# A dense GELU layer with its gradients: w1's second part issued earlier, dummy products in the head, and the first block's outputs taken out in another order

## The chip, the cores and the metric

The kernel runs on one core of a Trainium2 chip. TensorE multiplies matrices into PSUM, VectorE and ScalarE work on tiles, GpSimd and SyncE issue most transfers; all of them run side by side and wait for each other through semaphores. The metric is the device time in microseconds (us) of one execution. The kernel before takes 278.68 us, the median of three runs (277.06 to 278.73).

## The reference

All arrays are bf16: x and grad_out are 2048 x 448, w1 is 448 x 1792, w2 is 1792 x 448, with biases b1 and b2.

```python
def _fwd_reference(x, w1, b1, w2, b2):
    h = jnp.einsum("bsd,df->bsf", x, w1) + b1
    h = _gelu(h)                                  # tanh approximation
    return jnp.einsum("bsf,fd->bsd", h, w2) + b2

_out, _vjp = jax.vjp(_f, x, w1, b1, w2, b2)
_grads = _vjp(grad_out)
return (_out, *_grads)
```

So there are six outputs: the layer's result, and the gradients of x, w1, b1, w2 and b2.

## The kernel before, in words

The rows are cut into four blocks of 512, the 1792 hidden columns into seven pairs of 128. The main loop (line 371) has 28 steps, `g` = 0 to 27, seven for each block; a step handles one pair in one block, with rows along the free axis.

For a step, `M1` (line 216) multiplies w1 by x into `u` in PSUM: six matmuls of 512 columns, three for each half of the pair. 448 is three times 128 and 64 more, and the products of these 64 are in `rest` (line 227), which runs them for `u` of the next step and for `q` of this one, in the order u, q, u, q. `M4` (line 240) is the other six matmuls of `q`, w2 transposed by grad_out. `act_first` (line 246) copies `u` with its bias to `V` (line 250), squares it (line 251) and takes the GELU to `hT` (line 252). `dve_first` (line 266) makes an argument for `act_second`'s tanh (line 270), `dve_second` (lines 274 to 277) builds the derivative of the GELU, and `dve_gate` (line 280) multiplies it with `q` into `ghT`. `u` and `q` have one buffer each. So M1 of a step can start when ScalarE has copied the step before, and `q` can be written when the gate before has read it.

The order of everything is written out by hand. Step 0 is prepared ahead of the loop: lines 365 to 370 are M1(0), its remainder, `first_step`, which shares step 0 between ScalarE and VectorE, and M1(1). In the loop, step g runs `rest` for g + 1 and g, M4(g), the gate, the first half of step g + 1, and then pieces of products that make outputs.

These products are `Unit`s (line 293): kind "o" is 128 rows of the layer's result, kind "g" 128 rows of x's gradient. A unit is fourteen matmuls of 448 columns (line 311), one for each 128 hidden columns, run as pieces between the other work. Its accumulator is one of four PSUM buffers `acc` taken in a ring. Block 0's four "o" units grow in steps 0 to 6, two pieces each a step (`grown`). Block 1's first two "o" units grow in steps 7 to 13; in these steps block 0's "g" units run too (`own`, eight pieces a step). When a unit is full, it is taken out either by VectorE, which adds b2 (line 327), or by ScalarE (line 325); a unit that ScalarE takes out has b2 added by one more matmul (line 313), of a row of ones by one row of b2. Which engine it is, line 297 says. Step 6 ends with a `flush` for ScalarE's units; VectorE's come in the next step, behind M4 and ahead of the gate (line 380). In step 7 M1(9) stands ahead of the pieces, in the other steps M1 stands behind them.

The loads of the first weights are lines 167 to 175. SyncE issues the transposed loads of x, grad_out and w2 (lines 139, 140, 144, 145, 155, 156), ScalarE b1 and the first 512 columns of w1 in two parts (lines 148 and 149, called at 169 and 171); between these two parts stands an activation of one element (line 170) that loads ScalarE's table. Before any data is there, TensorE runs eight products of zeros (line 178), brings b1 onto partitions by fourteen small products (line 182), and runs one more product of zeros (line 185).

Behind the loop come the last block's units, then the column sums for the biases, then the gradients of w1 (lines 463 and 471) and w2 (line 482), which are nothing but matmuls and copies.

Of the kernel before, what the change touches and what calls it, by code (L numbers as in the profile page):

```python
# [10 lines left out]
BF16 = mybir.dt.bfloat16  # L11
# [7 lines left out]
def kernel(  # L19
# [15 lines left out]
    nc = tc.nc  # L35
    P = 128
    B, S, D = x.shape
# [23 lines left out]
    const = ctx.enter_context(tc.tile_pool(name="const", bufs=1))  # L61
# [22 lines left out]
    T_flat = const.tile([P, 4 * 2 * SB], BF16, name="T")  # L84
    b2_bc = const.tile([P, D], BF16, name="b2_bc")
    b1_col = const.tile([P, NF], F32, name="b1_col")
    ones_r = const.tile([1, P], BF16, name="ones_r")

    w1_sb = w1_flat.rearrange("p (k f) -> p k f", k=KD)
    w2T_sb = w2T_flat.rearrange("p (k f) -> p k f", k=KD)  # L90
# [8 lines left out]
    def xq(b):  # L99
        o = (b % 2) * 2 * KD * SB  # L100
        return xg_flat[:, o:o + KD * SB].rearrange("p (k s) -> p k s", k=KD)

    def gq(b):
        o = ((b % 2) * 2 + 1) * KD * SB
        return xg_flat[:, o:o + KD * SB].rearrange("p (k s) -> p k s", k=KD)
# [5 lines left out]
    def hT(g):  # L111
        return ring(hT_flat, HR, g)

    def ghT(g):
        return ring(ghT_flat, GR, g)
# [21 lines left out]
    def load_x(b):  # L137
        rows = slice(b * SB, (b + 1) * SB)
        nc.sync.dma_start_transpose(out=xq(b)[:, 0:KF, :], in_=x2[rows, DL:D])
        nc.sync.dma_start_transpose(out=xq(b)[:, KF, :], in_=x2[rows, 0:P])  # L140

    def load_g(b):
        rows = slice(b * SB, (b + 1) * SB)
        nc.sync.dma_start_transpose(out=gq(b)[:, KF, :], in_=g2[rows, DOV:D])
        nc.sync.dma_start_transpose(out=gq(b)[:, 0:KF, :], in_=g2[rows, 0:DM])

    def load_w1(eng, f0, f1):
        eng.dma_start(out=w1_sb[:, 0:KF, f0:f1], in_=w1[DL:D, f0:f1].rearrange("(k p) f -> p k f", p=P))
        eng.dma_start(out=w1_sb[0:DL, KF, f0:f1], in_=w1[0:DL, f0:f1])
# [13 lines left out]
    b1_row = T_flat[0:1, 4 * SB:4 * SB + F]  # L163
    nc.vector.memset(warm, 0.0)
    nc.vector.memset(ones, 1.0)
    nc.vector.memset(ones_r[:], 1.0)
    load_x(0)
    nc.scalar.dma_start(out=b1_row, in_=b1.rearrange("(o f) -> o f", o=1))
    load_w1(nc.scalar, 0, 256)
    nc.scalar.activation(out=T_flat[0:1, SB + 2:SB + 3], in_=ones, func=ACT.Gelu_apprx_tanh)  # L170
    load_w1(nc.scalar, 256, 512)
    load_g(0)
    load_w2T(0, 256)
    load_w2(nc.sync, 0, 2)
    load_w1(nc.sync, 512, 768)
    pw = psum_a.tile([P, SB], F32, name="acc")
    for i in range(8):
        nc.tensor.matmul(pw[:], lhsT=warm[:, 0:P], rhs=warm, start=True, stop=True)

    pb = psum_a.tile([P, SB], F32, name="acc")  # L180
    for ft in range(NF):
        nc.tensor.matmul(pb[:, ft:ft + 1], lhsT=b1_row[:, ft * P:(ft + 1) * P], rhs=ones, start=True, stop=True)
    nc.vector.tensor_copy(out=b1_col[:], in_=pb[:, 0:NF])
    for i in range(1):
        nc.tensor.matmul(pw[:], lhsT=warm[:, 0:P], rhs=warm, start=True, stop=True)
    load_w2T(256, 512)
    load_w2(nc.sync, 2, 4)
# [18 lines left out]
    def blk(g):  # L206
        return divmod(g, NPAIR)

    def cols(g, h):
        c = g % NPAIR  # L210
        return slice((2 * c + h) * P, (2 * c + h + 1) * P)
# [4 lines left out]
    def M1(g):  # L216
        if g == 0:
            u_of[g] = [psum_a.tile([P, SB], F32, name="acc")[:] for h in range(2)]
        else:
            u = psum_u.tile([P, 2, SB], F32, name="u")  # L220
            u_of[g] = [u[:, h, :] for h in range(2)]
        for h in range(2):
            for kt in range(KF):
                nc.tensor.matmul(u_of[g][h], lhsT=w1_sb[:, kt, cols(g, h)], rhs=xq(g // NPAIR)[:, kt, :],  # L224
                                 start=(kt == 0), stop=False, skip_group_check=True)

    def rest(gu, gg):

        if gg is not None:
            q = psum_g.tile([P, 2, SB], F32, name="q")  # L230
            g_of[gg] = q
        for h in range(2):
            if gu is not None:
                nc.tensor.matmul(u_of[gu][h], lhsT=w1_sb[0:DL, KF, cols(gu, h)], rhs=xq(gu // NPAIR)[0:DL, KF, :],  # L234
                                 start=False, stop=True, tile_position=(0, 0), skip_group_check=True)
            if gg is not None:
                nc.tensor.matmul(q[:, h, :], lhsT=w2T_sb[DL:P, KF, cols(gg, h)], rhs=gq(gg // NPAIR)[DL:P, KF, :],
                                 start=True, stop=False, tile_position=(DL, 0), skip_group_check=True)

    def M4(g):  # L240
        for h in range(2):
            for kt in range(KF):
                nc.tensor.matmul(g_of[g][:, h, :], lhsT=w2T_sb[:, kt, cols(g, h)], rhs=gq(g // NPAIR)[:, kt, :],  # L243
                                 start=False, stop=(kt == KF - 1), skip_group_check=True)

    def act_first(g):
        u = u_of.pop(g)
        for h in range(2):
            ft = 2 * (g % NPAIR) + h
            nc.scalar.activation(out=V_of(g)[:, h, :], in_=u[h], func=ACT.Identity, bias=b1_col[:, ft:ft + 1])  # L250
        nc.scalar.activation(out=A_of(g), in_=V_of(g), func=ACT.Square, scale=math.sqrt(3.0 * GELU_C * GELU_A))  # L251
        nc.scalar.activation(out=hT(g), in_=V_of(g), func=ACT.Gelu_apprx_tanh)  # L252
# [13 lines left out]
    def dve_first(g):  # L266
        nc.vector.scalar_tensor_tensor(out=B_of(g), in0=A_of(g), scalar=3.0 * GELU_C, in1=V_of(g), op0=ALU.add, op1=ALU.mult)  # L267
# [11 lines left out]
    def dve_gate(g):  # L279
        nc.vector.scalar_tensor_tensor(out=ghT(g), in0=t_of(g), scalar=1.0, in1=g_of.pop(g)[:], op0=ALU.add, op1=ALU.mult)  # L280
# [12 lines left out]
    class Unit:  # L293
        def __init__(self, kind, b, j):
            self.kind, self.b, self.j, self.done, self.ps = kind, b, j, 0, None

            self.by_act = kind == "g" or (b == 0 and j >= 2)

        def piece(self):
            ft = self.done  # L300
            c, h = divmod(ft, 2)
            g = self.b * NPAIR + c
            if self.ps is None:
                self.ps = psum_a.tile([P, SB], F32, name="acc")
            js = slice(self.j * P, (self.j + 1) * P)
            if self.kind == "o":
                lhsT, rhs = hT(g)[:, h, js], w2_sb[:, ft, :]
            else:
                lhsT, rhs = ghT(g)[:, h, js], w1T_sb[:, ft, :]
            bias = self.by_act and self.kind == "o"  # L310
            nc.tensor.matmul(self.ps[:, 0:D], lhsT=lhsT, rhs=rhs, start=(ft == 0), stop=(ft == NF - 1 and not bias))  # L311
            if bias and ft == NF - 1:
                nc.tensor.matmul(self.ps[:, 0:D], lhsT=ones_r[:], rhs=b2_bc[0:1, :], start=False, stop=True)
            self.done += 1
            return self.done == NF

# [18 lines left out]
    def run_pieces(units):  # L335
        for un in units:
            if un.piece():
                full.append(un)

    def flush(by_act=None):  # L340
        for un in [un for un in full if by_act in (None, un.by_act)]:
            full.remove(un)
            evict(un)
# [27 lines left out]
    for g in range(NSTEP):  # L371
        b, c = blk(g)
        pieces = [U[k] for k in seq[b] for _ in range(NF)]
        n = len(pieces)
        own = pieces[n * c // NPAIR:n * (c + 1) // NPAIR]
        grown = [U[k] for k in grow[b] for _ in range(2)]
        nxt = g + 1 if g + 1 < NSTEP else None
        rest(nxt, g)
        M4(g)
        flush(False)  # L380
        dve_gate(g)
        if nxt is not None:
            act_first(nxt)
        flush(True)
        if nxt is not None:
            dve_first(nxt)
        last = b == 0 and c == NPAIR - 1
        if last:
            run_pieces(grown + own)
            flush(True)  # L390
        if nxt is not None:
            act_second(nxt)
            dve_second(nxt)
        if g == NPAIR:
            M1(g + 2)
        if not last:
            run_pieces(grown + own)
        if g != NPAIR and g + 2 < NSTEP:
            M1(g + 2)
        for _ in range(2):  # L400
            if g >= NPAIR - 1 and stored < g:
                store_h(stored)
                stored += 1
        if c == 2 and 0 < b < NB - 1:
            load_x(b + 1)
            load_g(b + 1)
        for t in turns.get(g, []):
            turn_gh(*t)
# [45 lines left out]
    for t0, t1 in ((0, 4), (4, HT)):  # L454
        n = (t1 - t0) * P
        for h in range(2):
            a0, a1 = t0 + h * HT, t1 + h * HT
            cs = slice(a0 * P, a1 * P)
            for kt in range(KF):
                ps = psum_a.tile([P, SB], F32, name="acc")  # L460
                psv = ps[:, 0:n].rearrange("p (t f) -> p t f", f=P)
                for st in range(NS):
                    nc.tensor.matmul(psv, lhsT=x_all[:, st, kt * P:(kt + 1) * P], rhs=gh_rows(st, a0, a1),  # L463
                                     start=(st == 0), stop=(st == NS - 1))
# [3 lines left out]
        for st in range(NS):  # L468
            for h in range(2):
                psv = ps[h * DL:(h + 1) * DL, 0:n].rearrange("p (t f) -> p t f", f=P)  # L470
                nc.tensor.matmul(psv, lhsT=x_all[:, st, KF * P:D], rhs=gh_rows(st, t0 + h * HT, t1 + h * HT),  # L471
                                 start=(st == 0), stop=(st == NS - 1), tile_position=(0, h * DL), skip_group_check=True)
# [49 lines left out]
```

## Time and profile before

| | |
|---|---|
| median of three runs | 278.68 us (277.06 to 278.73) |
| the profiled execution, its own time | 278.49 us |
| its span from first to last instruction | 276.7 us |
| granted TensorE clock, mean | 0.993 |
| TensorE busy | 269.0 us, 97% |
| VectorE busy | 189.0 us, 68% |
| ScalarE busy | 144.2 us, 52% |
| GpSimd busy | 50.7 us, 18% |

Times inside the profile are counted from the span's start. PE is TensorE's matmuls, PEld its weight loads, DVE VectorE, ACT ScalarE, POOL GpSimd, SP SyncE; a "q" behind a name is the engine's queue of transfers. A matmul's end is modelled and overlaps the start of the next, so the distance between two starts is the better measure of what one costs.

### The profile page before, as it was taken

Reading aid. Unit: us, or ns where it says so; the run is one execution under the profiler, and the core shown is the slowest. Engines: PE = TensorE matmul, PEld = TensorE weight load, DVE = VectorE, ACT = ScalarE, POOL = GpSimd, SP = SyncE. Lnnn points to the kernel's source line nnn. Section 1 sums busy time; section 2 is a strip of 40 time slices with the busy share of each in tenths; the row PEclk is TensorE's granted clock in tenths of the full one; section 3 lists DMA queues with packets and bytes.
Section 4 is the critical chain, followed back from the end, with each engine's and each line's share of the span. In section 5 each row is a group of like instructions: output and inputs, shape, how many; then the busy total and the mean of one; then the engine's idle time right before and its main releaser. Section 6 shows DMA issues by size and latency. Waiting matters only on the chain.

```text
span 276.7 us, 3585 instructions
## 1 busy us (share of the span) xinstructions
PE 269.0 (97%) x1401; PEld 123.6 (45%) x1401; DVE 189.0 (68%) x218; ACT 144.2 (52%) x188; POOL 50.7 (18%) x54
## 2 busy tenths in 40 slices
PE   8799999899999999999999999999999999999994
PEld 3144443344444444444444445554444655555552
DVE  0679999999999999899888781129999980000000
ACT  2597888788878877888667750021111211112111
POOL 0000000840120503031130234211700019400000
PEclk9799999999999999999999999999999999999999
DMA  7989999999789965435635329999999961101110
GB/s 147 189 206 177 218 142 224 237 326 227 135 223 182 263 79 114 71 113 112 175 121 78 109 71 218 309 341 250 196 185 262 246 88 57 42 10 50 50 52 33
DMA packets 101763, 43.78 MB, mean 158 GB/s; under 512 B 90353, under 2 KB 98353, under 8 KB 101746
## 3 DMA queue, kind: packets, MB, share of 16 engines
q1 hardware_dynamic: 94272, 26.68, 52.6%
q0 software_dynamic: 4448, 14.69, 16.4%
q10 hardware_dynamic: 3026, 2.18, 2.9%
q8 instruction: 11, 0.18, 0.3%
q14 instruction: 6, 0.05, 0.1%
HBM read 7.00 MB, written 14.23 MB: 77 GB/s over the span
## 4 chain that ended last, share of the span: by engine, by line
PE 81%; DVE 12%; SPq 4%; DMA 1%; ACT 0%; issue 0%; DVEq 0%
PE acc L311 27%; PE acc L482 15%; PE acc L463 13%; PE q L243 10%; PE u L224 9%; PE u L234 4%; DVE Bt L267 3%; DVE T L274 3%; DVE ghT_h L280 3%; PE acc L471 2%; DVE T L277 2%; DVE T L275 1%; DMA w_gw<-in_w_dram 1%; SPq L155 1%; SPq L156 1%; DVE T L276 1%
## 5 line engine op out<-in xcount | busy, mean ns | idle before, releaser
L311 PE MATMUL acc<-w_gw,hT_h 128*128 128x448 bf16 x224 | 46.1, 352 | 0.0
L311 PE MATMUL acc<-w1T_gw,ghT_h 128*128 128x448 bf16 x224 | 45.2, 352 | 0.0
L224 PE MATMUL u<-xg_h,w_x 128*128 128x512 bf16 x162 | 40.7, 388 | 3.0 <-DMA w_x<-in_w_dram 2.0
L250 ACT ACTIVATE VA<-u,b_col 128x512 f32<-128x512 f32 x54 | 34.1, 681 | 17.3 <-PE u L234 16.6
L280 DVE SCALAR_TENSOR_TENSOR ghT_h<-T,q 128x1024 bf16<-128x1024 bf16 x28 | 34.2, 1221 | 10.8 <-PE q L243 9.7
L243 PE MATMUL q<-xg_h,w2T_g 128*128 128x512 bf16 x168 | 41.1, 381 | 0.0
L463 PE MATMUL acc<-gh_nat,w_x 128*128 128x512 bf16 (+1 forms) x192 | 36.7, 353 | 0.0
L270 ACT ACTIVATE T<-Bt 128x1024 bf16<-128x1024 f32 x28 | 29.6, 1056 | 11.8 <-DVE Bt L267 11.7
L274 DVE SCALAR_TENSOR_TENSOR T<-VA,hT_h 128x1024 bf16<-128x1024 f32 x28 | 34.1, 1218 | 0.2 <-ACT hT_h L264 0.2
L267 DVE SCALAR_TENSOR_TENSOR Bt<-VA 128x1024 f32<-128x1024 f32 x27 | 32.9, 1218 | 0.0
L311 PEld LDWEIGHTS <-hT_h 128*128 128x128 bf16 x224 | 21.8, 98 | 21.6 <-issue 0.2
L311 PEld LDWEIGHTS <-ghT_h 128*128 128x128 bf16 x224 | 21.9, 98 | 20.8
L448 DVE TENSOR_TENSOR VA<-VA,gh_nat 128x1792 f32<-128x1792 f32 x14 | 30.0, 2142 | 0.5
L251 ACT ACTIVATE VA<-VA 128x1024 f32<-128x1024 f32 x27 | 28.5, 1057 | 0.9
L252 ACT ACTIVATE hT_h<-VA 128x1024 bf16<-128x1024 f32 x27 | 28.1, 1041 | 0.0
L224 PEld LDWEIGHTS <-w_x 128*128 128x128 bf16 x168 | 16.7, 100 | 22.9 <-issue 3.5
L463 PEld LDWEIGHTS <-w_x 128*128 128x128 bf16 x192 | 18.7, 98 | 17.8 <-issue 0.4
L243 PEld LDWEIGHTS <-w2T_g 128*128 128x128 bf16 x168 | 14.1, 97 | 25.4 <-issue 12.2
L484 ACT CAST w_gw<-acc 128x448 bf16<-128x448 f32 x13 | 6.9, 533 | 32.6 <-PE acc L482 32.6
L331 POOL DMA_DIRECT2D out_dram<-io_o x8 | 6.0, 748 | 96.2 <-DVE io_o L327 48.3
L465 ACT CAST w1T_gw<-acc 128x512 bf16<-128x512 f32 (+1 forms) x12 | 6.3, 533 | 30.1 <-PE acc L463 23.9
L284 POOL DMA_DIRECT2D hT_dram<-hT_h x28 | 20.4, 729 | 0.7 <-ACT hT_h L252 0.7
(55 smaller groups left out, 230.4 us busy)
## 6 DMA issues: line engine op xcount, KB each, us to landing
hT_dram<-hT_h POOLq DMA_DIRECT2D x28, 256.0 KB, 3.9
out_dram<-io_o POOLq DMA_DIRECT2D x8, 224.0 KB, 4.6
out_dram<-io_g POOLq DMA_DIRECT2D x8, 224.0 KB, 2.9
w_x<-in_x_dram POOLq DMA_DIRECT2D x1, 1792.0 KB, 11.1
w2T_g<-in_grad_out_dram POOLq DMA_DIRECT2D x1, 1792.0 KB, 15.0
out_dram<-w_gw SPq DMA_DIRECT2D x4, 336.0 KB, 2.4
w_x<-in_w_dram SPq DMA_DIRECT2D x2, 384.0 KB, 3.7
out_dram<-w1T_gw ACTq DMA_DIRECT2D x2, 384.0 KB, 5.2
```

The source lines that it names most:

```text
L224: nc.tensor.matmul(u_of[g][h], lhsT=w1_sb[:, kt, cols(g, h)], rhs=xq(g // NPAIR)[:, kt, :], start=(kt == 0), stop=False, skip_group_check= ...
L243: nc.tensor.matmul(g_of[g][:, h, :], lhsT=w2T_sb[:, kt, cols(g, h)], rhs=gq(g // NPAIR)[:, kt, :], start=False, stop=(kt == KF - 1), skip_ ...
L250: nc.scalar.activation(out=V_of(g)[:, h, :], in_=u[h], func=ACT.Identity, bias=b1_col[:, ft:ft + 1])
L251: nc.scalar.activation(out=A_of(g), in_=V_of(g), func=ACT.Square, scale=math.sqrt(3.0 * GELU_C * GELU_A))
L267: nc.vector.scalar_tensor_tensor(out=B_of(g), in0=A_of(g), scalar=3.0 * GELU_C, in1=V_of(g), op0=ALU.add, op1=ALU.mult)
L270: nc.scalar.activation(out=t_of(g), in_=B_of(g), func=ACT.Tanh, scale=-1.0 / 3.0)
L274: nc.vector.scalar_tensor_tensor(out=p_of(g), in0=A_of(g), scalar=GELU_C, in1=hT(g), op0=ALU.add, op1=ALU.mult)
L280: nc.vector.scalar_tensor_tensor(out=ghT(g), in0=t_of(g), scalar=1.0, in1=g_of.pop(g)[:], op0=ALU.add, op1=ALU.mult)
L311: nc.tensor.matmul(self.ps[:, 0:D], lhsT=lhsT, rhs=rhs, start=(ft == 0), stop=(ft == NF - 1 and not bias))
L448: nc.vector.tensor_tensor(out=gsb_v, in0=gsb_v, in1=gh_rows(st, 0, NF), op=ALU.add)
L463: nc.tensor.matmul(psv, lhsT=x_all[:, st, kt * P:(kt + 1) * P], rhs=gh_rows(st, a0, a1), start=(st == 0), stop=(st == NS - 1))
L482: nc.tensor.matmul(ps[:, 0:D], lhsT=h_blk[ft][:, st, :], rhs=g_all[:, st, :], start=(st == 0), stop=(st == NS - 1))
```

## The change

Five edits, none of which changes what is computed.

1. The second part of w1 (columns 256 to 511) is issued by ScalarE directly behind the first; the one-element activation follows both.
2. In the head there are seven products of zeros and, behind b1, three, instead of eight and one. In step 0 four more products, of w1 by x, stand between `rest` and M4(0); nothing reads their result.
3. b2 is added by a product over all 128 partitions: a tile of 1/128 by b2 as it stands on every partition, instead of a row of ones by one row.
4. In block 0 ScalarE takes out units 0 and 1, VectorE units 2 and 3; it was the other way round.
5. In step 7 the pieces of block 1's two "o" units run ahead of M1(9), those of the "g" unit behind it; before, all ran behind it.

```diff
-    ones_r = const.tile([1, P], BF16, name="ones_r")
+    w128 = const.tile([P, P], BF16, name="w128")
...
-    nc.vector.memset(ones_r[:], 1.0)
+    nc.vector.memset(w128[:], 1.0 / P)
...
     load_w1(nc.scalar, 0, 256)
+    load_w1(nc.scalar, 256, 512)
     nc.scalar.activation(out=T_flat[0:1, SB + 2:SB + 3], in_=ones, func=ACT.Gelu_apprx_tanh)
-    load_w1(nc.scalar, 256, 512)
...
-    for i in range(8):
+    for i in range(7):
         nc.tensor.matmul(pw[:], lhsT=warm[:, 0:P], rhs=warm, start=True, stop=True)
...
-    for i in range(1):
+    for i in range(3):
         nc.tensor.matmul(pw[:], lhsT=warm[:, 0:P], rhs=warm, start=True, stop=True)
...
-            self.by_act = kind == "g" or (b == 0 and j >= 2)
+            self.by_act = kind == "g" or (b == 0 and j < 2)
...
-                nc.tensor.matmul(self.ps[:, 0:D], lhsT=ones_r[:], rhs=b2_bc[0:1, :], start=False, stop=True)
+                nc.tensor.matmul(self.ps[:, 0:D], lhsT=w128[:], rhs=b2_bc[:], start=False, stop=True)
...
         rest(nxt, g)
+        if g == 0:
+
+            for i in range(4):
+                nc.tensor.matmul(pw[:], lhsT=w1_sb[:, 0, 0:P], rhs=xq(0)[:, 0, :], start=True, stop=True)
         M4(g)
...
         if g == NPAIR:
+            run_pieces(grown)
             M1(g + 2)
-        if not last:
+            run_pieces(own)
+        elif not last:
             run_pieces(grown + own)
```

## The prediction

> **What bounds the kernel now.** I read the shares of the chain of waits first, then the chain in order of time, then TensorE's waits. Columns of the chain: start, duration, what.
>
> ```profile
> PE 81%; DVE 12%; SPq 4%; DMA 1%; ACT 0%; issue 0%; DVEq 0%
> ```
> ```profile
> 16.31 1.21 DVE Bt L267
> ...
> 45.60 1.22 DVE ghT_h L280
> ...
> 49.53 0.69 ACT VA L250
> ...
> 50.26 1.46 PE u L224 x6
> ...
> 53.98 0.32 PE u L234
> ...
> 273.18 0.53 ACT w_gw L490
> ```
> ```profile
> PE u L224 <- DMA w_x<-in_w_dram: 2.0, 1, 2.0
> PE u L224 <- ACT VA L250: 0.9, 1, 0.9
> ```
>
> The run has three parts. Up to 16.3 us is the head: loads, and step 0. From 16.3 to 49.5 VectorE carries the chain (block 0). From 50.26 to 273.2 TensorE carries it without a break. So a microsecond counts if it comes off the time at which VectorE starts to run without a pause, off the handover near 50, or off TensorE's list after 50.26. TensorE itself waits twice for something a program can move: 2.0 us in the head, 0.9 us at the handover. Now the head as a timeline (start, duration, engine, line; in brackets the idle time before and what ended it):
>
> ```profile
> 2.35 1.28 ACT L170 ACT_TABLE_LOAD   x1 [2.35 <-issue]
> 3.64 0.20 ACT L170 ACTIVATE T<-T 1x1 bf16<-1x1 bf16 x1
> 5.27 0.17 DVE L183 COPY b_col<-acc 128x14 f32<-128x14 f32 x1 [4.01 <-PE acc L182]
> 5.33 0.44 ACTq L148 DMA_DIRECT2D w_x<-in_w_dram  x1
> 5.57 1.99 PE L224 MATMUL acc<-xg_h,w_x 128*128 128x512 bf16 x6
> 6.00 0.15 PEld L224 LDWEIGHTS <-w_x 128*128 128x128 bf16 x1 [0.28 <-issue]
> 6.43 1.45 SPq L155 DMA_TRANSPOSE w2T_g<-in_w_dram  x1
> 7.49 0.60 PE L234 MATMUL acc<-xg_h,w_x 64*128 64x512 bf16 x2
> 7.92 0.69 ACT L257 ACTIVATE VA<-acc,b_col 128x512 f32<-128x512 f32 x1 [4.07 <-PE acc L234]
> 7.93 1.28 SPq L156 DMA_TRANSPOSE w2T_g<-in_w_dram  x1
> 10.15 2.74 PE L224 MATMUL u<-xg_h,w_x 128*128 128x512 bf16 x6 [2.05 <-DMA w_x<-in_w_dram]
> 10.64 1.04 ACT L270 ACTIVATE T<-Bt 128x1024 bf16<-128x1024 f32 x1
> 12.70 0.69 DVE L277 TENSOR_TENSOR T<-T 128x1024 bf16<-128x1024 bf16 x1
> 12.82 0.61 PE L234 MATMUL u<-xg_h,w_x 64*128 64x512 bf16 x1
> 13.66 1.47 PE L243 MATMUL q<-xg_h,w2T_g 128*128 128x512 bf16 x6
> 14.96 1.30 PE L311 MATMUL acc<-w_gw,hT_h 128*128 128x448 bf16 x6
> 15.16 1.22 DVE L280 SCALAR_TENSOR_TENSOR ghT_h<-T,q 128x1024 bf16<-128x1024 bf16 x1 [1.77 <-PE q L243]
> ```
> ```profile
> 7.50:10.00 2.50, 0.60 (x3) 0.10 (x2) 1.45 (x3) 2.05 (x4) 0.00 (x0) 1.00 1.31 208
> 10.25:13.25 3.00, 3.00 (x10) 0.76 (x9) 2.79 (x5) 1.43 (x2) 0.00 (x0) 0.50 0.86 201
> 13.50:16.50 3.00, 3.00 (x17) 1.40 (x16) 1.34 (x2) 2.65 (x4) 0.00 (x0) 1.00 0.81 183
> ```
>
> VectorE has step 0's factors ready at 12.70 + 0.69 = 13.39, and the gate of step 0 (line 280) starts at 15.16: it idles 1.77 us for `q`. Backwards, `q` is late because M1(1) (line 224) waited for w1's second part to 10.15 and then ran at the half clock: in the windows (the last three figures are the granted clock, the DMA engines' share and GB/s) TensorE is busy 0.60 of 2.50 us before 10, and the clock is 0.50 from 10.25 to 13.25 and 1.00 from 13.50. Six matmuls took 2.67 us there (10.15 to 12.82); M4(0) took 1.30 (13.66 to 14.96), or 0.217 each.
>
> **The change, part by part.** *Second part earlier.* Its issue at 5.33 took 4.8 us to the release at 10.15. Directly behind the first part it goes out when the table load of line 170 now starts, at 2.35; with the same 4.8 us it lands near 7.2. M1(0) and its remainder run to 7.49 + 0.43 = 7.9, so M1(1) follows with no gap, up to about 9.4. Its 448 x 256 values of two bytes are 0.23 MB, at the 208 GB/s of the first window 1.1 us of transfers, which now compete with x's first load; that may land later by 1.1 us at most, and by nothing if its own transfers go first. M1(0) begins at 6.0 in any case, next point, so I take 0.1. ScalarE's table load moves behind two more issues of 0.5 us; its next work is at 7.92, after 4.07 idle, which hides it.
>
> *Warm matmuls, 7 + 3 for 8 + 1.* One more ahead of M1(0), at the 0.43 us between 5.57 and 6.00. M1(0) has six matmuls in 7.49 - 5.57 = 1.92 us, less than 6 x 0.43 = 2.6: the clock rose during it. If it rises at the same moment, one slow matmul fewer remains in M1(0) and half the 0.43 comes back. Ends 0 (x late anyway) and 0.43; I take 0.25 for this and the 0.1 together. So step 0's factors are ready at 13.39 + 0.25 = 13.64.
>
> *Four products between the remainders and M4(0).* They sit in front of what the gate waits for. The remainders alternate u, q, u, q in TensorE's order, and q needs w2's first transposed piece, M4(0) the second:
>
> ```profile
> L155 SPq DMA_TRANSPOSE w2T_g<-in_w_dram x1: 1452/1452/1452, 6.4 to 6.4; - x1
> DMA to landing us min/median/max: 4.5/4.5/4.5
> ```
> ```profile
> L156 SPq DMA_TRANSPOSE w2T_g<-in_w_dram x5: 1282/1282/1292, 12.3 to 27.4; - x5
> DMA to landing us min/median/max: 3.0/3.7/4.5
> ```
>
> The first lands at 6.43 + 4.5 = 10.9, the second, by its five later siblings, at 7.93 + 3.0 to 4.5 = 10.9 to 12.4. So after M1(1) TensorE waits from about 9.6 to 10.9. Remainders: 0.84 at half clock (12.82 to 13.66), so 0.45 at full, to 11.35; four products at 0.217 = 0.87, to 12.2; M4(0) 1.30, to 13.5; then the 0.20 from 14.96 to 15.16, so the gate at 13.7. Against 13.64 that is level. Without the four it would be VectorE's 13.64 too: at full clock they cost 0.1 or nothing. I set the gate at 13.7: **head -1.45 us** (15.16 - 13.7). VectorE's next, line 267, needs step 1's Square: V(1) can start when tanh ends, 10.64 + 1.04 + 0.25 = 11.9, and the two copies (1.25, row of 48.96 below) and the Square (taken as tanh's 1.04, of as many columns) end at 14.2, under a gate that ends at 13.7 + 1.22 = 14.9. In block 0 the other loads keep SP's own pace, and TensorE needs less of a step than VectorE (1.30 + 0.45 + 1.30 and eight pieces at 0.19, by the rows at 51.55 and 52.30 below, make 4.6, and VectorE's step is (45.60 - 15.16) / 6 = 5.07), so the shift reaches 49.5 whole.
>
> *b2 by a full product; the memset.* Two matmuls of as many columns:
>
> ```profile
> L313 PE MATMUL acc<-b_bc,ones_r 1*128 1x448 bf16 x2 | 0.7, 358 | 0.0
> ```
> Cost 0, at most 0.3 us either way, under VectorE's chain. The larger memset lies in the 4.01 us in which VectorE waits for its first copy (row of 5.27).
>
> *Units 0 and 1 out by ScalarE, and the order of step 7.*
>
> ```profile
> 47.08 0.95 ACT L325 CAST io_o<-acc 128x448 bf16<-128x448 f32 x2
> 48.96 1.25 ACT L250 ACTIVATE VA<-u,b_col 128x512 f32<-128x512 f32 x2
> 51.55 0.92 PE L311 MATMUL acc<-w_gw,hT_h 128*128 128x448 bf16 x4
> 52.30 1.68 PE L311 MATMUL acc<-w1T_gw,ghT_h 128*128 128x448 bf16 x8
> ```
>
> Block 1's first two units take the accumulators that units 0 and 1 leave. VectorE frees those only behind step 7's M4; ScalarE frees its pair at 47.08 + 0.95 = 48.03. With the pairs swapped the four pieces of 52.30 - 51.55 = 0.75 us can run where TensorE now idles 0.92 us for V(8) (48.96 + 1.25 = 50.21), and M1(9) starts as before at V(8)'s end. Everything behind it comes **0.75 us** earlier. ScalarE makes the same two copies, VectorE the same two; the eight pieces of `g` wait for unit 2's buffer, which VectorE frees within 1.15 us of copying while M1(9) runs (1.29 us, 50.26 to 51.55). Ends: 0, if the pieces find no accumulator, and 0.92, the whole idle time.
>
> **Sum.** -1.45 - 0.75 = -2.2 us on the profiled execution's 278.49 (span 276.7): 276.3. The median of the runs is 278.68, 0.2 above it; one of the three had 277.06.
>
> **Two rules weighed.** By the windows the clock is 0.50 behind a stretch in which TensorE was busy for a quarter, and 1.00 some 3 us later. The Trainium skill, "TensorE: Matmul & The Clock Gate", Part 1: The HAM clock gate, says that the gate looks at windows of 3.4 us which run free of the kernel's start. The rows agree with it; by it the phase of a run, which no edit sets, moves the head, as in rivals B and C. The windows' DMA share is 1.31 from 7.50 to 10.00. The Trainium skill, "DMA: Bandwidth & Descriptors", Issuing engines are not separate DMA queues, says that loads issued from several engines interleave on the same 16; it speaks against the change, since w1's second part would then delay x by its share. By that rule alone, x would land at 6.4 for 5.3, M1(0) start 0.3 later than I take, and the sum be 276.6.
>
> **The rivals.** *B, the clock rises earlier.* If it is full when the three later warm matmuls run (half price, 0.65 for 1.3), M1(0) starts at about 5.4 and lasts 1.3: step 0's first copy at about 7.1 for 7.92. Then VectorE's 12.6 is the floor and M4(0) must come by it, which needs both w2 pieces about 1 us earlier, for which the lighter queue after 7.2 speaks. Head -2.6, sum 275.1 to 275.9. *C, the clock rises later, or falls in the wait from 9.6 to 10.9.* At 0.43 the four products take 1.7; with the clock back at 13.4 as now, M4(0) ends at 14.8 and the gate starts at 15.0: head -0.2, sum 277.5. Against it: in the stretch of 3.4 us before 10 TensorE would be busy for about 3. *D, the part does not go earlier.* It went out at 5.33, though ScalarE was done at 3.84, and x's first load landed then:
>
> ```profile
> L139 SPq DMA_TRANSPOSE xg_h<-in_x_dram x1: 1371/1371/1371, 0.7 to 0.7; - x1
> DMA to landing us min/median/max: 4.6/4.6/4.6
> ```
> 0.7 + 4.6 = 5.3. So the issue itself seems to have waited for that landing; why, no view shows. If the wait goes with the issue, M1(1) stays at 10.15 and the four products put 0.87 ahead of M4(0): head +0.87, handover -0.75, sum 278.6. *E, slower: the four products at half clock throughout.* From 10.9: remainders 0.84, products 1.7, M4(0) 2.6, and 0.2: gate at 16.2, head +1.1; sum 278.8, and 279.8 if w2's pieces land 1 us later still. It decides against the change once the gate starts after 15.16 + 0.75 = 15.9.
>
> **How the numbers follow.** A (the sum, 275.9 to 277.0) 0.46; B 0.25; C (277.0 to 278.3) 0.17; D 0.05; E 0.05; 0.02 for what I do not see. The time is A's, 276.3. The range leaves out the lowest of B and the top of C with D and E: 275.2 to 278.0. One per cent, about what a measurement of this kernel can tell from no change, is 2.8 us: faster is under 275.9, so B and the edge of A, 0.31; slower is above 281.5, a sliver of E and the unseen, 0.05; the rest 0.64.
>
> **What would show it.** After: ScalarE's second w1 issue near 2.4; TensorE without the 2.0 us wait; the clock at 1.00 from 10 on; the gate of step 0 near 13.7 with little idle before it; the chain's handover near 48.8, TensorE without the 0.9 us wait, and the remainder of step 9 at about 51.8 for 53.98. It would be wrong if the second part's issue stays at 5.3, if the clock column shows 0.50 behind 10, or if the four pieces of step 7 still stand behind M1(9).

## The result, and the profile after

The changed kernel takes 276.15 us, the median of six runs (275.92 to 276.47); the kernel before, run beside it, 278.13 us over six runs (277.06 to 278.73). The ratio is 0.9935, with a 95% interval of [0.991, 0.996]. The profiled execution took 276.47 us with a span of 274.7, 2.0 less than before. The forecast was 276.3.

TensorE's waits in the changed kernel, the longest two that a program can move:

```profile
PE acc L311 <- DMA w_gw<-in_w_dram: 1.1, 1, 1.1
PE u L224 <- ACT VA L250: 0.6, 1, 0.6
```

The 2.0 us for w1 are gone. A wait of 1.1 us for w2's rows is new. It lies in step 2 and costs nothing in this execution, as VectorE carries the chain there, but it uses up time that TensorE had in hand: 0.6 us are left, its wait at the handover. The head as a timeline (start, duration, engine, line):

```profile
2.34 0.68 ACTq L148 DMA_DIRECT2D w_x<-in_w_dram  x1
...
6.00 2.00 PE L224 MATMUL acc<-xg_h,w_x 128*128 128x512 bf16 x6
6.77 1.24 SPq L155 DMA_TRANSPOSE w2T_g<-in_w_dram  x1
7.93 0.60 PE L234 MATMUL acc<-xg_h,w_x 64*128 64x512 bf16 x2
...
8.36 0.69 ACT L257 ACTIVATE VA<-acc,b_col 128x512 f32<-128x512 f32 x1 [3.26 <-PE acc L234]
8.46 1.47 PE L224 MATMUL u<-xg_h,w_x 128*128 128x512 bf16 x6
...
10.40 1.04 PE L382 MATMUL acc<-xg_h,w_x 128*128 128x512 bf16 x4
...
11.28 1.46 PE L243 MATMUL q<-xg_h,w2T_g 128*128 128x512 bf16 x6
...
13.13 0.69 DVE L277 TENSOR_TENSOR T<-T 128x1024 bf16<-128x1024 bf16 x1
...
13.93 1.22 DVE L280 SCALAR_TENSOR_TENSOR ghT_h<-T,q 128x1024 bf16<-128x1024 bf16 x1
```

The second issue of line 148 stands at 2.34 for 5.33. M1(1) follows M1(0)'s remainder at 8.46, six matmuls in 1.41 us (to 9.87, where the remainders begin) for 2.67. M4(0) is through at 12.6, and the gate of step 0 starts at 13.93 for 15.16, 0.1 behind VectorE's own factors (13.13 + 0.69 = 13.82). The same windows as before, with the granted clock third from the end:

```profile
7.50:10.00 2.50, 2.50 (x13) 0.73 (x13) 1.02 (x2) 1.61 (x3) 0.00 (x0) 1.00 0.78 159
10.25:13.25 3.00, 3.00 (x18) 1.21 (x15) 2.79 (x6) 3.00 (x4) 0.00 (x0) 1.00 0.74 185
```

TensorE is busy throughout, and the clock, which was 0.50 in the second window, is 1.00. The handover, in the chain of the changed kernel (start, duration, what):

```profile
44.37 1.22 DVE ghT_h L280
...
48.29 0.69 ACT VA L250
...
49.02 1.46 PE u L224 x6
50.47 1.51 PE acc L311 x8
51.99 0.32 PE u L234
```

Between M1(9) and the next remainder the chain holds eight pieces where twelve stood. The remainder's row in the chain is at 51.99 for 53.98. So the whole 2.0 us between the two profiled executions is won by then: 15.16 - 13.93 = 1.23 in the head, and 0.75 for the four pieces.

### The profile page after: what moved, and what is told of

Read it like the earlier page. It is cut to its first block, busy times and chain, and to the rows that moved or that the text cites. A ratio compares the mean times of both kernels' runs of the same rounds, so it can differ in the third digit from the quotient of the medians.

```text
span 274.7 us, 3594 instructions
## 1 busy us (share of the span) xinstructions
PE 268.3 (98%) x1406; PEld 123.9 (45%) x1406; DVE 188.9 (69%) x218; ACT 143.8 (52%) x188; POOL 50.7 (18%) x54
## 4 chain that ended last, share of the span: by engine, by line
PE 83%; DVE 13%; ACT 1%; issue 1%; DVEq 0%
PE acc L311 27%; PE acc L488 15%; PE acc L469 13%; PE q L243 10%; PE u L224 9%; PE u L234 4%; DVE T L274 3%; DVE Bt L267 3%; DVE ghT_h L280 3%; PE acc L477 2%; DVE T L277 2%; DVE T L275 1%; PE acc L178 1%; DVE T L276 1%; PE acc L224 1%
## 5 line engine op out<-in xcount | busy, mean ns | idle before, releaser
L224 PE MATMUL u<-xg_h,w_x 128*128 128x512 bf16 x162 | 39.4, 379 | 0.6 <-ACT VA L250 0.6
```

## The experiments

Each kernel was timed in five rounds beside the kernel before, twelve runs each. The kernel before was timed in three such groups, 35 runs each. It spread widely: its medians were 277.43, 278.20 and 278.35, with runs from 276.39 to 280.35. Kernels with the early load stayed within 0.4 us of their medians, but for two runs of one of them.

The spread goes with the granted clock. Every run has its mean granted clock on record, and the 105 runs of the kernel before fall into three groups by it. At 0.999 or 1.000 there are 44 runs, with a median of 276.82 us (276.39 to 277.47, and three from 278.3 to 278.8). At 0.993 or 0.994 there are 58, with a median of 278.56 (277.96 to 279.37). At 0.988 there are three, from 280.04 to 280.35. The profiled execution of the kernel before is of the second kind: 0.993, with some 3 us at half clock. So kernels with the early load are compared by their medians, and kernels with the late load by the rows of their profiles and by their runs against those of the kernel before that were timed beside them and had the same granted clock.

**The load alone.**

```diff
     load_w1(nc.scalar, 0, 256)
+    load_w1(nc.scalar, 256, 512)
     nc.scalar.activation(out=T_flat[0:1, SB + 2:SB + 3], in_=ones, func=ACT.Gelu_apprx_tanh)
-    load_w1(nc.scalar, 256, 512)
```

> The kernel before with the first edit alone: w1's second part issued by ScalarE right behind the first. Theory S (the load carries the head): the issue goes out near 2.3, M1(1) follows M1(0) without a gap at full clock, the gate of step 0 starts at 13.4 to 13.6 for 15.16, and the time is 1.5 us under the kernel before. Rival K (the products that keep the array busy carry the head): without them the clock falls to half in a wait near 10 us, M4(0) ends late and the gain is under 0.5 us. Rival D (the issue waits for x's landing wherever it stands): issue at 5.3, no gain.

Measured: 276.66 us (276.40 to 276.89), ratio 0.9972 [0.9951, 0.9993]. Its timeline:

```profile
7.84 1.47 PE L224 MATMUL u<-xg_h,w_x 128*128 128x512 bf16 x6
...
10.75 1.47 PE L243 MATMUL q<-xg_h,w2T_g 128*128 128x512 bf16 x6 [0.71 <-DMA w2T_g<-in_w_dram]
12.51 0.69 DVE L277 TENSOR_TENSOR T<-T 128x1024 bf16<-128x1024 bf16 x1
13.30 1.22 DVE L280 SCALAR_TENSOR_TENSOR ghT_h<-T,q 128x1024 bf16<-128x1024 bf16 x1
```

The gate is at 13.30, 1.86 us earlier, with no product added. The clock did not fall although TensorE waits 0.71 us ahead of M4(0). The profiled execution of 276.62 us is 1.87 under that of the kernel before. K and D fall. S holds for the head, but not with its 1.5 us for the time: the medians differ by 0.77 us. By granted clock, all twelve runs stand at 0.998 or above, and their median is 1.91 under the 16 runs of the kernel before at 0.993 or 0.994 (278.57), and only 0.08 under its 19 runs at 0.999 or 1.000 (276.74). So the early load wins what the half clock cost, and next to nothing where the clock had stayed up. The rows of before say the same: with M1(1) from 10.15 at full clock, an estimate is 10.15 + 1.30 + 0.45 for the remainders + 1.30 + 0.20 = 13.4 for the gate, where VectorE's own factors were ready at 13.39. So the wait of 2.0 us by itself would have been covered or nearly so; the half clock behind it was not.

**The products alone.**

```diff
-    for i in range(8):
+    for i in range(7):
...
-    for i in range(1):
+    for i in range(3):
...
         rest(nxt, g)
+        if g == 0:
+            for i in range(4):
+                nc.tensor.matmul(pw[:], lhsT=w1_sb[:, 0, 0:P], rhs=xq(0)[:, 0, :], start=True, stop=True)
         M4(g)
```

> The kernel before with the second edit alone: 7 + 3 products of zeros for 8 + 1, and the four products ahead of M4(0); w1's second part is still issued behind the activation. Theory S: M1(1) still starts near 10.15 at half clock, the four products (0.22 to 0.43 us each) push M4(0) and the gate of step 0 to 16.0 or later, and the time is 0.5 to 1.3 us above the kernel before. Rival K: the clock is kept and the time falls by about 1 us.

Measured: 277.72 us (276.85 to 280.11), ratio 1.0039 [1.001, 1.0068].

```profile
10.80 2.74 PE L224 MATMUL u<-xg_h,w_x 128*128 128x512 bf16 x6 [2.37 <-DMA w_x<-in_w_dram]
...
14.11 1.04 PE L382 MATMUL acc<-xg_h,w_x 128*128 128x512 bf16 x4
...
16.48 1.22 DVE L280 SCALAR_TENSOR_TENSOR ghT_h<-T,q 128x1024 bf16<-128x1024 bf16 x1 [2.75 <-PE q L243]
```

The wait for w1 and the half clock behind it stay, and the four products stand between them and M4(0): the gate is at 16.48. The products do not pay by themselves; they cost. The eight runs with a clock of 0.997 or more have a median 0.85 us above that of the kernel before's 19, the price of four products (4 x 0.217 = 0.87), and the other four are 1.4 us above its 16.

**The changed kernel without the four products.**

```diff
         rest(nxt, g)
-        if g == 0:
-            for i in range(4):
-                nc.tensor.matmul(pw[:], lhsT=w1_sb[:, 0, 0:P], rhs=xq(0)[:, 0, :], start=True, stop=True)
         M4(g)
```

> The changed kernel without the four products ahead of M4(0). Theory S: the gate of step 0 waits for VectorE's own factors in both, so it starts at 13.8 to 13.9 here too, and the time is that of the changed kernel within 0.2 us. Rival K: with TensorE idle from 10.4 to 11.3 the clock falls in the next window, M4(0) or the matmuls behind it run at half rate, and about 1 us of the gain is lost.

Measured: 275.95 us (275.83 to 276.32), ratio 0.9937 [0.9914, 0.996]. TensorE waited 0.95 us for w2's second piece where the four had stood, at full clock. The changed kernel's 276.15 is within 0.2, though the two were timed apart; the next two kernels, timed together, differ in the four products alone and take 276.11 with them and 276.15 without. So they neither help nor hurt.

**8 + 1 products of zeros in the changed kernel.**

```diff
-    for i in range(7):
+    for i in range(8):
...
-    for i in range(3):
+    for i in range(1):
```

> The changed kernel with 8 + 1 products of zeros in the head, as before the change, for 7 + 3. Theory S: M1(0) starts at 5.57 for 6.00, as x's and w1's first loads have landed by 5.4; step 0's factors and the gate come 0.2 to 0.4 us earlier, and the time is 0.2 to 0.4 us under the changed kernel's 276.15, so 275.75 to 275.95. Rival (x lands later because w1's second part competes): M1(0) waits, same time. Rival K (the longer warm stretch secures the clock): 0.5 us or more slower in part of the runs.

Measured: 276.11 us (275.86 to 276.31), ratio 0.9933 [0.9903, 0.9963]: the same, so S fell here. In its profile the remainder of M1(0) waits 0.47 us for x's second load; the next kernel shows it in full.

**Neither the four nor 7 + 3.** This is the last kernel with its four products taken out too.

> The changed kernel with 8 + 1 products of zeros and without the four products ahead of M4(0): so the load, the handover and the b2 product alone. Theory S: these carry all of the gain; the time is that of the kernel with 8 + 1 and the four, within 0.1 us, or 0.2 to 0.4 us under the changed kernel. Rival K: without any of the added products the clock falls in part of the runs, which then take 1 us more.

Measured: 276.15 us (275.92 to 276.41), ratio 0.9931 [0.9905, 0.9958]. So edit 2 as a whole is worth nothing beside the early load. In its timeline M1(0) starts early and its remainder waits:

```profile
5.61 1.45 PE L224 MATMUL acc<-xg_h,w_x 128*128 128x512 bf16 x6
7.79 0.59 PE L234 MATMUL acc<-xg_h,w_x 64*128 64x512 bf16 x2 [0.72 <-DMA xg_h<-in_x_dram]
8.20 0.69 ACT L257 ACTIVATE VA<-acc,b_col 128x512 f32<-128x512 f32 x1 [3.10 <-PE acc L234]
```

The remainder needs x's second transposed load. Here are that load's rows in the kernel before, then in the changed kernel (the load alone has the 5.1 too):

```profile
L140 SPq DMA_TRANSPOSE xg_h<-in_x_dram x1: 1238/1238/1238, 2.2 to 2.2; - x1
DMA to landing us min/median/max: 4.0/4.0/4.0
```
```profile
L140 SPq DMA_TRANSPOSE xg_h<-in_x_dram x1: 1238/1238/1238, 2.2 to 2.2; - x1
DMA to landing us min/median/max: 5.1/5.1/5.1
```

The same load takes 1.1 us longer with w1's second part beside it (5.1 to 5.6 us in the profiles with the early load), and lands at 7.3 or later. That is the new floor of the first step: starting M1(0) sooner brings the wait, not the end, forward. The rule weighed before (the Trainium skill, "DMA: Bandwidth & Descriptors", Issuing engines are not separate DMA queues) agrees with this trace: 5.1 us for 4.0. It struck x's second load, where the forecast had looked at the first, which took 4.7 us for 4.6.

**No product of zeros at all.** As the last kernel, and both loops of zeros left out too.

```diff
-    for i in range(8):
+    for i in range(0):
...
-    for i in range(1):
+    for i in range(0):
```

> The kernel with the early load, the handover and the b2 product, and now without any product of zeros in the head and without the four ahead of M4(0). Theory S (the clock follows TensorE's own busy time in free windows of 3.4 us): M1(0) starts at 5.6 at half clock and takes 2.6 us, the first copy comes near 9 for 8.2, the gate of step 0 near 14.6 to 15, and the time is 0.8 to 1.5 us above the same kernel with 8 + 1 products (276.15). Rival (x's second load is the floor of the first step anyway): within 0.3 us of it.

Measured: 277.00 us (276.77 to 277.19), ratio 0.9953 [0.9934, 0.9973]: 0.85 us above the same kernel with 8 + 1, which was timed apart from it; the two profiled executions differ by 0.69 us, their gates by 0.68 (14.45 for 13.77).

```profile
5.59 2.72 PE L224 MATMUL acc<-xg_h,w_x 128*128 128x512 bf16 x6 [2.88 <-DMA xg_h<-in_x_dram]
8.24 1.03 PE L234 MATMUL acc<-xg_h,w_x 64*128 64x512 bf16 x2
...
9.20 2.60 PE L224 MATMUL u<-xg_h,w_x 128*128 128x512 bf16 x6
...
14.45 1.22 DVE L280 SCALAR_TENSOR_TENSOR ghT_h<-T,q 128x1024 bf16<-128x1024 bf16 x1
```

M1(0) takes 2.65 us (5.59 to 8.24), six times 0.44, so it runs at half clock from end to end; with 8 + 1 it began at 5.61 and took 1.45. So some products of zeros are worth 0.7 to 0.85 us; nine or ten in either split brought M1(0) to full clock, wholly or in part, in the profiles with the whole part early.

**The handover alone.**

```diff
-            self.by_act = kind == "g" or (b == 0 and j >= 2)
+            self.by_act = kind == "g" or (b == 0 and j < 2)
...
         if g == NPAIR:
+            run_pieces(grown)
             M1(g + 2)
-        if not last:
+            run_pieces(own)
+        elif not last:
             run_pieces(grown + own)
```

> The kernel before with the fourth and fifth edits alone: units 0 and 1 out by ScalarE, and in step 7 block 1's two o units ahead of M1(9). Theory S: the head as before (gate of step 0 near 15.2), TensorE's wait for V(8) falls from 0.9 to about 0.2 us, the remainder of step 9 comes 0.75 us earlier against M1(9)'s start (2.9 for 3.65 us), and the time is 0.7 us under the kernel before. Rival R (the lead is given back in block 1, where VectorE's gate then holds TensorE): no change at the end.

Measured: 277.73 us (275.53 to 278.00), ratio 0.9996 [0.997, 1.0022]; by the medians of all runs nothing can be told, as the head keeps its wait and its spread. By granted clock, the nine runs at 0.994 have a median 0.76 us under that of the kernel before's 16, and the three at 1.000 are 0.68 under its 19. By the profile, TensorE's wait for V(8) is 0.16 us, and from M1(9) at 50.41 to the remainder at 53.31 it is 2.90 us, for 3.65. With the gate at 15.34 for 15.16 the span is 276.1 for 276.7: -0.75 and +0.18. The lead is not given back later, so R falls.

**The swap of units alone, and the order alone.** The first and the second hunk of the last diff.

> The kernel before with the fourth edit alone: ScalarE takes out units 0 and 1 of block 0, VectorE 2 and 3; M1(9) still stands ahead of all pieces of step 7. Theory S (the handover's 0.75 us needs both edits): the four pieces still run behind M1(9), so from M1(9) to the remainder of step 9 it is 3.65 us as in the kernel before, and the time is the kernel before's within 0.2 us. Rival T (the earlier accumulators alone bring the gain): 0.5 us or more faster.

> The kernel before with the fifth edit alone: in step 7 block 1's two o units run ahead of M1(9), while VectorE still takes out units 0 and 1. Theory S: the pieces wait for accumulators that VectorE frees only behind its own work of step 7 (near 51.1 and 51.6 on the time line of the kernel before), M1(9) stands behind them and starts near 52 for 50.26, the remainder of step 9 comes near 54.9 for 53.9, and the time is about 1 us above the kernel before. Rival: no change, because TensorE would have waited for V(8) anyway.

Measured: the swap 278.16 us (276.52 to 278.77), ratio 0.9995 [0.9964, 1.0026], and 3.66 us from M1(9) at 50.25 to the remainder at 53.91, as before: nothing. The order alone took 276.93 us (275.63 to 279.31), ratio 0.9954 [0.992, 0.9988]; its six runs at 1.000 and its five at 0.994 are 0.77 and 0.81 us under the kernel before's of the same clock, the handover's whole gain. S held for the first and fell for the second. The order alone, as a timeline:

```profile
47.11 0.95 ACT L325 CAST io_o<-acc 128x448 bf16<-128x448 f32 x2
...
49.20 0.92 PE L311 MATMUL acc<-w_gw,hT_h 128*128 128x448 bf16 x4
50.28 1.46 PE L224 MATMUL u<-xg_h,w_x 128*128 128x512 bf16 x6 [0.16 <-ACT VA L250]
50.52 1.15 DVE L327 TENSOR_TENSOR io_o<-acc,b_bc 128x448 bf16<-128x448 f32 x2
```

The four pieces run at 49.20, before VectorE takes out units 0 and 1 at 50.52. They cannot be using those accumulators; they use the pair that ScalarE freed at 47.11 to 48.06, whichever units it held.

**All four units out by VectorE, with the new order.**

```diff
-            self.by_act = kind == "g" or (b == 0 and j >= 2)
+            self.by_act = kind == "g"
```

> The kernel before with the fifth edit (block 1's two o units ahead of M1(9) in step 7), and with VectorE taking out all four units of block 0; b2 then needs no product. It asks whose accumulator the pieces of step 7 use. Theory U (they take whichever pair is freed first, and need that ScalarE frees a pair in step 6): now none is free before VectorE's step 7 work, the four pieces and M1(9) behind them wait to about 51, TensorE waits 1 us or more there, and the time is 0.7 to 1.5 us above the kernel before's runs of the same clock. Rival (the pieces need no freed accumulator): TensorE's wait stays under 0.3 us and the time is 0.7 us under the kernel before.

Measured: 280.97 us (278.14 to 282.14), ratio 1.0097 [1.0064, 1.013].

```profile
50.46 2.21 DVE L327 TENSOR_TENSOR io_o<-acc,b_bc 128x448 bf16<-128x448 f32 x4
51.13 1.07 PE L311 MATMUL acc<-w_gw,hT_h 128*128 128x448 bf16 x4 [2.29 <-DVE io_o L327]
52.04 2.62 PE L224 MATMUL u<-xg_h,w_x 128*128 128x512 bf16 x6
```
```profile
48.80:52.20 3.40, 1.11 (x6) 0.48 (x5) 3.37 (x8) 3.37 (x5) 0.28 (x1) 1.00 1.05 108
52.20:55.50 3.30, 3.30 (x10) 1.22 (x8) 3.30 (x4) 0.55 (x2) 2.97 (x5) 0.50 1.16 312
```

Theory U holds. Its four runs at 0.994 are 1.2 us above the kernel before's of that clock, as expected. The median of all twelve is 2.6 us above, as seven of them stand at 0.988, and of the 105 runs of the kernel before only three do. With no pair freed in step 6, the pieces wait 2.29 us for VectorE. TensorE is then busy 1.11 of 3.40 us, and the clock is 0.50 for the next 3.3 us, a second such stretch after the one in the head: M1(9) takes 2.4 us (52.04 to 54.46) for 1.3.

**b2 by one row in the changed kernel.**

```diff
-                nc.tensor.matmul(self.ps[:, 0:D], lhsT=w128[:], rhs=b2_bc[:], start=False, stop=True)
+                nc.tensor.matmul(self.ps[:, 0:D], lhsT=ones_r[:], rhs=b2_bc[0:1, :], start=False, stop=True)
```

> The changed kernel with the third edit undone: b2 by a row of ones and one row of b2. The two products lie under VectorE's chain in step 6. Theory S: 276.1, the changed kernel's time within 0.2 us. Rival: the one-row products break TensorE's stream for 0.3 us each, push the remainder of step 8 and show at the end: 0.3 us or more slower.

Measured: 276.40 us (275.90 to 277.90), ratio 0.9936 [0.9912, 0.996]. TensorE's wait for w2's rows, then step 7 in this kernel, ScalarE's copy first and then TensorE:

```profile
PE acc L311 <- DMA w_gw<-in_w_dram: 1.5, 1, 1.5
```
```profile
47.55 1.25 ACT L250 ACTIVATE VA<-u,b_col 128x512 f32<-128x512 f32 x2
```
```profile
43.23 0.36 PE L313 MATMUL acc<-b_bc,ones_r 1*128 1x448 bf16 x1
43.52 0.55 PE L311 MATMUL acc<-w_gw,hT_h 128*128 128x448 bf16 x2
...
48.29 0.92 PE L311 MATMUL acc<-w_gw,hT_h 128*128 128x448 bf16 x4
49.05 1.24 PE L224 MATMUL u<-xg_h,w_x 128*128 128x512 bf16 x5
```

V(8) is done at 47.55 + 1.25 = 48.80, but M1(9) follows the pieces at 49.05, 0.25 us later, where the changed kernel has 0.05: here TensorE itself is late, by 0.2 us. In step 6 the ten products take 2.31 us (42.75 to 45.06) for 1.89 in the changed kernel (42.40 to 44.29), as one row each costs 0.29 to the next start, for 0.19, and the products around them a little more too. That makes 0.42 us, less than the 0.58 that TensorE had in hand in the changed kernel. It shows here because w2's rows came later as well: step 2's pieces start at 23.77 for 23.34. In the chain of this kernel TensorE carries everything from there on. So the one-row products cost 0.2 us in this execution, and by the same rows nothing in the changed kernel's. The medians differ by 0.25 us, but the two kernels were not run side by side, and the two profiled executions have the same span, 274.7.

**Half of w1's second part early.** The kernel with neither the four nor 7 + 3, and:

```diff
-    load_w1(nc.scalar, 256, 512)
+    load_w1(nc.scalar, 256, 384)
     nc.scalar.activation(out=T_flat[0:1, SB + 2:SB + 3], in_=ones, func=ACT.Gelu_apprx_tanh)
+    load_w1(nc.scalar, 384, 512)
```

> As the kernel with the early load, the handover and the b2 product (8 + 1 products of zeros, no four; 276.15), but only half of w1's second part (columns 256 to 383) goes out ahead of the activation, the other half (384 to 511) behind it. Theory S with contention as the floor: x's second load then lands earlier than 7.5 to 7.75, M1(0)'s remainder follows M1(0) without the 0.5 to 0.7 us wait, and the time falls by 0.2 to 0.6 us to 275.6 to 275.9; M1(1)'s second half may wait to 10 at no cost, as q has 1 us in hand. Rival: the second half's issue waits for x's landing and comes after 10.5, M4(0) is late, no gain or a loss.

Measured: 277.77 us (277.57 to 278.32), ratio 0.9993 [0.9972, 1.0014]; the rival. In the rows of this kernel every line of the loop is one further down:

```profile
4.89 0.21 ACT L171 ACTIVATE T<-T 1x1 bf16<-1x1 bf16 x1
5.91 2.72 PE L225 MATMUL acc<-xg_h,w_x 128*128 128x512 bf16 x6
7.90 0.37 ACTq L148 DMA_DIRECT2D w_x<-in_w_dram  x1
8.56 1.03 PE L235 MATMUL acc<-xg_h,w_x 64*128 64x512 bf16 x2
9.44 0.47 ACTq L149 DMA_DIRECT2D w_x<-in_w_dram  x1
10.02 0.69 ACT L258 ACTIVATE VA<-acc,b_col 128x512 f32<-128x512 f32 x1 [4.92 <-PE acc L235]
```

ScalarE is done at 5.1, yet the second half goes out at 7.90 and 9.44. grad_out's two loads land then: 3.45 + 4.4 = 7.85 and, of the second, 4.75 + 4.7 = 9.45. No view shows what these issues waited for; that it is the landings is argued from the times, which agree within 0.05 us, as at 5.3 in the kernel before. The first copy stands behind these issues on ScalarE, at 10.02. With no products of zeros it followed such a remainder after 8.88 - 8.24 = 0.64 us, which would be 9.20 here: the issues cost it 0.8 us. So an issue that is held up delays the engine's other work too. It is mechanism D of the forecast, in a place where it does occur. The gate is at 15.60 for 13.77 in the kernel with the whole part early. The other 1.0 us of that is not the issue's: M1(0) and its remainder ran at half clock (M1(0) from 5.91 to 8.56). Why they did, with 8 + 1 products ahead of them, stays open. And theory S finds no support: x's second load took 5.3 us with only half of the bytes beside it, no less than with all of them (5.1 to 5.6), so its price did not follow the bytes.

## Why the prediction was right, point by point

- *Second part earlier*: right. Issue at 2.34 for the 2.35 predicted, M1(1) with no gap, the clock at 1.00 behind 10 us. The load alone gives the head's gain, as the run with it alone shows. The forecast started from an execution with the half clock and noted that the phase of a run moves the head, but it did not put a price on it: beside runs of the kernel before without the half clock, the same edit is worth 0.1 us.
- *Warm matmuls*: mis-sized. Step 0's factors moved by 13.82 - 13.39 = 0.43 us for the 0.25 taken. M1(0) started at 6.00 as predicted, but the clock rose one matmul later than in the profiled execution before, so nothing of the 0.43 came back. Nor is the term a cost of edit 2: with 8 + 1 the remainder waits for x's second load instead (0.47 us), and the time is the same.
- *Four products*: right that they cost about nothing, for a reason that differed. The forecast let the remainders wait for w2's first piece to 10.9; in fact that load took 2.7 us for 4.5 (issued at 6.77, landed at 9.5), with w1's second part out of its way (2.7 with the load alone too), and M4(0) was done 0.9 us earlier than forecast. So the gate was set by VectorE alone, at 13.93 for 13.7.
- *b2*: within the 0.3 us that were allowed, and the cover that was named, VectorE's chain, is thinner than it was. Once the four pieces fill TensorE's wait, TensorE has 0.58 us left there; the one-row products take 0.42 of it, and in the execution where w2's rows came 0.43 us later they stood out by 0.2. So edit 3 saves 0 to 0.2 us in this company.
- *Units and order of step 7*: the 0.75 us is right to the hundredth, but the step "block 1's first two units take the accumulators that units 0 and 1 leave" failed. They take the pair that is freed first. The order alone brings the gain, the swap nothing, so edit 4 was not needed for it.
- *The sum*: -1.23 - 0.75 = -1.98 for -2.2, on 278.49, which gives 276.5, the profiled execution's 276.47. That the forecast is only 0.15 from the median is luck in part: the sum was 0.2 too large, and the profiled execution, the longest of the six, lies 0.3 above their median. Rival D did not come about in the changed kernel, and does in the half-early one. Rival B did not come about either: no kernel with the early load has a median under 275.95. x's second load is in its way, and behind it w2's rows, which leave TensorE 0.58 us at the handover in the changed kernel, and 0.17 where the gate came at 13.35 (the kernel without the four). Rival C's clock at half does appear near 11 us in the kernels with the late load, but in none with the early one.

What stays open is what the runs of the kernel before at 0.999 or 1.000 look like, as none of them was profiled. Their granted clock leaves no room for 3 us at half speed behind w1's wait; why the clock fell in some runs and not in others is not shown.

## What to carry to other kernels

A wait of 2 us for a load can be covered by other work and still cost 2 us through the clock, so look for the load that ends an idle stretch of TensorE, and issue that load earlier before adding products that only keep the array busy. When a kernel's runs spread, sort them by the granted clock before comparing medians. An issue that is moved on an engine's queue can lengthen the transfers in flight (5.1 us for 4.0 here) and may wait for an earlier landing; look up the landing of every load near it, and what else the engine has behind it. When an edit removes slack, ask again about the costs that the slack had hidden, and about the next load in line.

## What the runs showed of the hardware

- The clock fell after stretches in which TensorE was not idle throughout: busy 1.46 of the 3.41 us before 10.05 in the kernel before, 1.11 of 3.40 us with all four units on VectorE. The Trainium skill, "TensorE: Matmul & The Clock Gate", Part 1: The HAM clock gate, has it fall after an idle window of about 3.4 us; here a busy third of one was not enough to hold it.
- The clock column of a profile is not to be believed ahead of the first change in it. With no products of zeros it reads 1.00 from 5.60 to 11.40 us,

```profile
5.60:11.40 5.80, 5.80 (x14) 1.54 (x13) 1.89 (x3) 2.49 (x4) 0.00 (x0) 1.00 0.95 179
```

  while M1(0) takes 0.44 us a matmul there, for 0.22 at full speed. The distance between matmuls tells it.
- The early load narrowed the spread of the runs: 276.39 to 279.36 us for the kernel before, 276.40 to 276.89 for the load alone, timed beside it.
